# Attention and gated block on one core: outputs transposed straight into the operand of wo, head sets in pairs, and the order of every engine moved by a table

## Chip, core and metric

The kernel runs on one core of one Trainium2 chip. The metric is the device time of one execution in microseconds; several executions are timed, and their median counts. One further execution is recorded by the hardware profiler; its span and rows are what this document quotes.

## What is computed

The reference, cut to what matters (S = 2048 tokens, D = 640, 32 heads of 20, F = 1536, bf16):

```python
mod = (silu(c) @ w_mod).reshape(1, 6, 1, -1)          # sa, ca, ga, sb, cb, gb
h = layernorm(x) * (1 + ca) + sa
q, k, v = split_heads(h @ wqkv)
o = softmax(q @ k.T / sqrt(20)) @ v                   # every head, 2048 x 2048 scores
x = x + ga * (merge_heads(o) @ wo)
h = layernorm(x) * (1 + cb) + sb
x = x + gb * (((h @ w_gate) * (h @ w_up)) @ w_down)
```

The exponentials are the bulk of ScalarE's work: 32 heads x 2048 x 2048.

## The kernel before

**A planner writes the program.** `build_kernel` makes tasks (engine, modelled duration, dependencies, buffers), `Sched.run` lays them out by an event model with priorities and gates, and `emit_program` (L356) writes one instruction stream for each engine in that order, with semaphore waits for dependencies on other engines. Each engine then runs its list strictly in order. Constants such as QUADS, STAGE, D_LEAD, HOLD, PVTOL or FILL_MIN steer the plan; STAGE holds overrides by head set.

**Tiling.** Queries go in seven chunks (CHUNKS: one of 512, six of 256). A chunk has eight head sets of four heads, so 56 items; the last is cut into two halves of 128 (SPLITJ), 57 in all. An item's scores are made in units of 128 partitions (keys) x 512 columns: 2048 units in all. The four heads of a set lie in the four strips of 32 rows of TensorE.

**Two ways through the softmax.** Most units go to ScalarE (ACT): a score visit of PE (L1524) writes two units into one of two PSUM sets of two banks, ACT takes the exponential of both at once (L1561, 128 x 1024) into PP, and PE multiplies by V (L2192). QUADS says how many groups of four units of each item go to VectorE (DVE) instead: DVE adds a bias and writes int16 (DB, L1585), then splits exponent and mantissa (L1617, L1625), and the product of the two parts is made by GpSimd (POOL) in four pieces (L1637) or by DVE (L1622); each such unit takes two value passes on PE instead of one. Their scores ride on score visits, in one of four other PSUM banks (G: 5, 6, 2, 7), which also take the projections, the value sums and all other rounds. The matmuls of such rounds have the lines of two helpers, L970 (four column strips of 32) and L966 (the whole array, in the last suffix).

```python
QUADS = ((0, 4, 3, 3, 3, 4, 4, 4), (2, 2, 1, 2, 2, 2, 1, 2), ...
```

**End of an item** (`item_end_tasks`, L1707 on): DVE transposes the value sums in blocks of 32 (L1717, OT), takes the reciprocal of the row sums (L1723), POOL or DVE normalizes (L1725, OTn), DVE transposes back (L1734, OcT), and four or five DMAs per item on SP's queue (L1746) copy the rows of each head to their places in Ocp, the left operand of wo:

```python
t = dma("sp", nr * n * 2, f, dps, prio=1.05 if j >= NSET - 2 else 2, dur=720.0)
```

wo is loaded by one DMA (L1492); the last head set of the last chunk is taken out of OcT instead, against a copy of its rows of wo in wo7 (four small DMAs, L1493).

**Suffix of a chunk** (`suffix`, L1773 on), spread by gates over the next chunk's score visits: product with wo (L1827), second layer norm, transposes (L1889), gate and up products by column blocks of 128 of F, with the two products of a block side by side in one bank (L1959 copies the gate product, L1966 multiplies), down product (L2062), output. Weights of gate and up stream through three staging buffers (stg, L1931).

**First part.** Layer norm and projections of Q, K, V run beside the first chunk's scores. K and most of Q are packed, written to DRAM and read back in strips of 32 rows (KT<-k_rows L1289, QT<-q_rows L1298), all on SP's queue.

**Fillers.** Where the plan has PE idle and its recent activity low, it puts in matmuls with no result: products with zeros into a value bank (L2523) or with the identity (L2551, L2553).

Of the kernel before, what the change touches and what calls it, by code (L numbers as in the profile page):

```python
# [13 lines left out]
SEM = 60.0  # L14
# [4 lines left out]
X_FIRST = 0.0  # L19
ACT_LAT = 250.0  # L20
# [16 lines left out]
LKTOL = 300.0  # L37


class Task:  # L40
    __slots__ = ("head", "hval", "hknow", "eng", "dur", "lat", "deps", "emits", "ctr", "prio", "gate", "acq", "on_start", "slots",
                 "start", "done", "needed", "val", "know", "nleft", "ready", "users", "name", "mode", "seq", "rt", "sem",
                 "nbytes", "cond", "alt", "land", "firm", "lk", "dead", "key")

    def __init__(self, eng, dur, emits, deps=(), ctr=None, prio=0.0, lat=None, gate=0, acq=(), on_start=None,
# [28 lines left out]
        self.dead = False  # L74
        if lat is None:
            lat = {"pe": PE_DRAIN, "act": ACT_LAT, "dve": DVE_LAT, "pool": 60.0}.get(eng, 0.0)
        self.lat = lat

# [5 lines left out]
class Slots:  # L84

    def __init__(self, ids, name=""):
        self.name = name
        self.free = [(i, []) for i in ids]
        self.hold = {}
        self.gone = set()  # L90
        self.out = {}

    def avail(self, only=None):
        best = None
        for k, (i, rel) in enumerate(self.free):
# [3 lines left out]
            for r in rel:  # L99
                t = max(t, r.done + SEM)  # L100
# [16 lines left out]
    def done(self, i, task):  # L117
        h = self.hold[i]
# [9 lines left out]
    def add(self, i, rel):  # L128
        self.free.append((i, rel))


class Sched:

    def __init__(self):
# [28 lines left out]
        self.lk_last = None  # L163

# [39 lines left out]
    def _enable(self, task):  # L204
        t = 0.0
        for d in task.deps:
            t = max(t, d.done + SEM)
        task.rt = t
        heapq.heappush(self.pend[task.eng], (t, task.seq, task))
# [68 lines left out]
    def step_engine(self, eng):  # L278
        if self.free_at[eng] > self.t:
            return False  # L280
        self.pull(eng)
        rl = self.readyl[eng]
        for k, task in enumerate(rl):
# [5 lines left out]
            if self.locked(eng, task):  # L289
                continue  # L290
            if self.acquire(task, self.t):
# [63 lines left out]

def emit_program(nc, sched, nsem_dma=56):  # L356
# [23 lines left out]
    for t in sched.all:  # L380
# [11 lines left out]
        for d in deps:  # L392
            if not (d.nbytes or d.eng != eng or d.eng in ("dve", "pool")):
                continue
            if d.head and eng == "act":
# [88 lines left out]
TB_GATE = 2  # L484
# [3 lines left out]
D_LEAD = 0.451  # L488
NB0, NSS = 3, 3
XB0, XSS = 0, 0  # L490
HEADG = 1000
OP_EARLY = 1
EV_OP = 0.5
# [3 lines left out]
LN2T = 0.6  # L497
# [5 lines left out]
HOLD = 110  # L503
PVTOL = 249
XDPRIO = 1.343
# [5 lines left out]
STX_G, STX_T, STX_S, W_ISSUE = 3, 20, 1.5, 600.0  # L511
ZFILL = 1
WD_POOL, WD_PRIO = 1, 400.0
# [4 lines left out]
WM_GATE = 8  # L518
# [3 lines left out]
K_LEAD = 0.683  # L522
# [3 lines left out]
D_LATE = 16  # L526
D_RES = 20
PVMIN, PVMAX, PVCAP = 2, 7, 12
PV0 = 0
V_PARTS = [[0, 2], [2, 4], [4, 6], [6, 8]]  # L530
V_L1 = 0.2
# [10 lines left out]
GATE_F = (0.446, 0.5, 0.5, 0.5, 0.5, 0.5, 1.0)  # L542
FILL_MIN = 4190.746
# [9 lines left out]
LN2P = 0.85  # L553
NALT = 1
OPFIRST = 1500
STG_B = 0.95
ENDP, END3, P_POW = 0.4, 1, -1.0
HT_L = 0.25
V_L = 0.221
LATE_A = 2.065  # L560
LATE_L = 1.418
LATEQ = (2, 3)
LATEQ_A = -20
LATEQ_F = 0.35
# [2064 lines left out]
```

## Time and profile before

| | |
|---|---|
| median of 3 runs | 805.1 us (804.75 to 807.88) |
| span of the profiled execution | 803.8 us |
| instructions | 37,761 |
| DVE busy | 697.8 us |
| POOL busy | 386.0 us |
| data moved by DMA | 64.66 MB |

A row of the groups reads: line, engine, operation, output<-input, shapes, count; then busy time and the mean nanoseconds of one; then idle time of the engine just before, and what ended it. A row of a source line reads: minimum, median and maximum duration, then the first and last start. A row of stretches reads: the stretch, its length, busy time and count for PE, weight loads (PEld), DVE, ACT and POOL, then granted clock, DMA share and GB/s. A row of the chain or of the timeline reads: start, duration, what. "SPq" is a DMA's issue on SP's queue. ACT's time of one exponential covers its way through the engine, so neighbours overlap; the step from start to start says how fast they follow each other.

### The profile page before, as it was taken

The page shows a single profiled execution, that of the slowest core. Times are in us where ns is not written, and L with a number is a line of the kernel's source. Part 1 is how long each engine was busy: PE and PEld are TensorE (multiplying, and loading weights), DVE is VectorE, ACT ScalarE, POOL GpSimd, SP SyncE. Part 2 cuts the span into 40 slices and gives each one's busy share as a digit, 9 for nine tenths or more (in the row PEclk, how much of TensorE's full clock was granted, in tenths as well). Part 3 has the DMA queues.
Part 4 walks back from the last instruction along what each step waited for, and adds up shares of the span by engine and source line. Part 5 has one row for each costly group of instructions (what it writes and reads, how often), then busy time and mean ns, then how long its engine had stood idle before and what let it go on. Part 6 is the DMA issues. An engine that isn't in the chain of part 4 may idle for free.

```text
span 803.8 us, 37761 instructions
## 1 busy us (share of the span) xinstructions
PE 790.4 (98%) x16595; PEld 380.6 (47%) x16595; DVE 697.8 (87%) x1401; ACT 764.8 (95%) x847; POOL 386.0 (48%) x396
## 2 busy tenths in 40 slices
PE   8999999999999999999999999999999999999998
PEld 4433433333244434445555455555555555555567
DVE  7978788799989999988999999999899988898754
ACT  6899899999999999999999999999999999999961
POOL 3347455654366565763444443545534554455300
PEclk9999999999999999999999999999999999999999
DMA  9733212212341532120032404231540254414420
GB/s 297 243 113 91 62 43 64 61 33 76 92 109 50 167 88 52 35 55 13 24 81 65 95 16 112 57 73 39 121 89 15 54 118 94 98 37 106 92 68 18
DMA packets 154314, 64.66 MB, mean 80 GB/s; under 512 B 116951, under 2 KB 154151, under 8 KB 154151
## 3 DMA queue, kind: packets, MB, share of 16 engines
q1 hardware_dynamic: 153223, 61.10, 30.0%
q8 instruction: 132, 2.16, 1.1%
q10 hardware_dynamic: 928, 1.15, 0.5%
q14 instruction: 31, 0.25, 0.1%
HBM read 50.63 MB, written 8.99 MB: 74 GB/s over the span
## 4 chain that ended last, share of the span: by engine, by line
PE 77%; ACT 14%; DVE 5%; issue 2%; DMA 1%; SPq 1%; POOL 0%; DVEq 0%; ACTq 0%
PE ps_all L1524 26%; PE ps_all L970 21%; PE ps_all L2192 19%; ACT PP L1561 14%; PE ps_all L1230 4%; PE ps_all L966 3%; DVE DB L1585 2%; PE ps_all L1889 1%; PE ps_all L1166 1%; PE ps_all L1127 1%; DVE DSS L1617 1%; PE ps_all L2523 0%; DVE DSS L1625 0%; DMA QT<-q_rows 0%; PE ps_all L991 0%
## 5 line engine op out<-in xcount | busy, mean ns | idle before, releaser
L1561 ACT ACTIVATE PP<-ps_all 128x1024 bf16<-128x1024 f32 x810 | 748.5, 1090 | 6.7 <-PE ps_all L1524 4.8
L1637 POOL TENSOR_TENSOR DSS<-DB,DSS 128x512 bf16<-128x512 bf16 x268 | 305.0, 1157 | 290.6 <-DVE DSS L1625 254.2
L1585 DVE TENSOR_SCALAR DB<-ps_all 128x512 int16<-128x512 f32 x428 | 285.5, 681 | 50.5 <-PE ps_all L1524 48.0
L1524 PE MATMUL ps_all<-QT,KT 32*128 32x256 bf16 (+2 forms) x3648 | 319.4, 287 | 4.5 <-DMA QT<-q_rows 0.8
L1524 PEld LDWEIGHTS ps_all<-QT,KT 32*128 32x128 bf16 x3648 | 93.9, 92 | 204.1 <-ACT PP L1561 141.5
L2192 PE MATMUL ps_all<-PP,Vf 128*32 128x256 bf16 (+2 forms) x2892 | 163.6, 291 | 0.5 <-DVE KPB L1242 0.3
L970 PE MATMUL ps_all<-h2T,stg 128*32 128x256 bf16 (+2 forms) x2716 | 122.9, 281 | 0.3 <-DVE DB L1585 0.2
L2192 PEld LDWEIGHTS ps_all<-PP,Vf 128*32 128x32 bf16 (+1 forms) x2892 | 54.5, 94 | 76.4 <-issue 67.6
L2192 PE MATMUL ps_all<-DSS,Vf 128*32 128x256 bf16 (+1 forms) x1512 | 88.7, 291 | 0.0
L1617 DVE TENSOR_SCALAR DSS<-DB 128x2048 int16<-128x2048 int16 x107 | 77.2, 722 | 0.8
L970 PEld LDWEIGHTS ps_all<-h2T,stg 128*32 128x32 bf16 x2716 | 61.6, 96 | 26.9 <-issue 22.0
L1625 DVE TENSOR_SCALAR DSS<-DB 128x2048 int16<-128x2048 int16 x107 | 73.2, 684 | 0.8 <-PE ps_all L2192 0.8
L970 PE MATMUL ps_all<-wd,hprod 128*32 128x320 bf16 (+1 forms) x1404 | 61.0, 277 | 0.0
L1725 POOL TENSOR_TENSOR OTn<-OT,invT 128x256 bf16<-128x256 f32 (+1 forms) x49 | 35.3, 721 | 37.7 <-DVE invT L1723 37.5
L1622 DVE TENSOR_TENSOR DSS<-DB,DSS 128x2048 bf16<-128x2048 bf16 x40 | 51.5, 1287 | 0.0
L2192 PEld LDWEIGHTS ps_all<-DSS,Vf 128*32 128x32 bf16 x1512 | 36.5, 95 | 20.9 <-issue 12.4
L970 PE MATMUL ps_all<-wV,hT 128*32 128x160 bf16 x1280 | 38.9, 236 | 0.9 <-DVE DB L1585 0.3
L970 PEld LDWEIGHTS ps_all<-wd,hprod 128*32 128x32 bf16 x1404 | 31.2, 96 | 14.2 <-issue 10.8
L1717 DVE STREAM_TRANSPOSE OT<-ps_all 128x256 f32<-128x256 f32 (+2 forms) x57 | 27.1, 475 | 8.8 <-PE ps_all L2192 8.5
L1230 PE MATMUL ps_all<-hT,wk 128*32 128x512 bf16 x360 | 32.3, 382 | 0.0
L970 PEld LDWEIGHTS ps_all<-wV,hT 128*32 128x32 bf16 x1280 | 24.6, 97 | 15.9 <-issue 8.2
L1230 PE MATMUL ps_all<-hT,wq 128*32 128x512 bf16 x375 | 31.3, 382 | 0.6 <-DVE OT L1717 0.6
(133 smaller groups left out, 556.1 us busy)
## 6 DMA issues: line engine op xcount, KB each, us to landing
stg<-in_B_w_gate_dram SPq DMA_DIRECT2D x74, 160.0 KB
stg<-in_B_w_up_dram SPq DMA_DIRECT2D x74, 160.0 KB
KT<-k_rows SPq DMA_DIRECT2D x112, 32.0 KB
QT<-q_rows SPq DMA_DIRECT2D x48, 64.0 KB
Ocp<-OcT SPq DMA_DIRECT2D x164, 10.0 KB
wm<-in_w_mod_dram SPq DMA_DIRECT2D x3, 800.0 KB
x<-in_A_x_dram SPq DMA_DIRECT2D x7, 320.0 KB
k_rows<-KPA SPq DMA_DIRECT2D x16, 128.0 KB
```

What stands on the lines that cost most here:

```text
L970: return lambda e, b: e.matmul(ps[32 * x:32 * x + 32, b, c0 + o:c0 + o + w], lhs()[:, 32 * x:32 * x + 32], rhs() if w == n else rhs()[:, o ...
L1230: f = [lambda e, b_, k=k, x=x: e.matmul(ps[x:x + min(32, w - x), b_, :], wx[:, k, r0 + x:r0 + min(x + 32, w)], hT[tc][:, k, :], tile_posit ...
L1524: ems.append(lambda e, i=i, kt=kt: e.matmul(dstf()[:, i * u.n:(i + 1) * u.n], KT[32 * u.s:32 * u.s + 32, u.j, kt * 128:(kt + 1) * 128], QT ...
L1561: return e.activation(PPs[g % 2][:, cellp["p"], 0:nu * 512], ps[:, b0:b0 + nu, :].rearrange("p b c -> p (b c)"), AFT.Exp, scale=ESCALE)
L1585: return e.tensor_scalar(DBl[st_["slot"]][:, x * 512:(x + 1) * 512], bank(cell["b"]), EBIAS, 0.0, op0=ALU.add, op1=ALU.max)
L1617: return e.tensor_scalar(DSl[st_["ss"][0]][:, :], DBl[st_["slot"]][:, :], 0x7F, 0x3F00, op0=ALU.bitwise_and, op1=ALU.bitwise_or)
L1622: return e.tensor_tensor(d, DBl[st_["slot"]][:, :].bitcast(BF16), d, ALU.mult)
L1625: return e.tensor_scalar(DSl[st_["ss"][1]][:, :], DBl[st_["slot"]][:, :], 0x7F80, 2, op0=ALU.bitwise_and, op1=ALU.bitwise_or)
L1637: return e.tensor_tensor(d, DBl[st_["slot"]][:, x * w:x * w + w].bitcast(BF16), d, ALU.mult)
L1717: t1 = Task("dve", n * 1.1 + 70, lambda e: e.transpose(OT[:, 0:n], ps[:, item_info[it]["bank"], 0:n].rearrange("p (b q r) -> p b r q", q=3 ...
L1725: f3 = lambda e: e.tensor_tensor(OTn[:, 0:n].rearrange("p (b c r) -> p b r c", c=32, r=2), OT[:, 0:n].rearrange("p (b r c) -> p b r c", c= ...
L2192: ems.append(lambda e, i=i, kt=kt, stt=stt, stp=stp: e.matmul(ps[32 * s:32 * s + mc, bk, 0:u.n], Vf[:, (kt * H + 4 * u.j + s) * VW:(kt * H ...
```

## The change

What it does, beside new constants all over:

- **Outputs.** OcT, wo7 and the DMAs into Ocp go. The normalization writes only the 20 real columns of each head, head set beside head set, into one OTn of 160 columns per group of 64 queries. Once 32 columns are full, one transpose of DVE writes a block of Ocp. The rows of Ocp then have another order, and wo is loaded in 48 pieces to match.
- **Pairs.** Two neighbouring head sets of 256 queries share one bank of value sums, 256 columns each, and one first transpose, one reciprocal and one second transpose.
- **Gate and up** of two column blocks share a bank (256 columns each): one copy and one product of 512 instead of two of 256. Staging buffers: five, two of which open during the first chunks.
- **Score visits** are made when they are placed, from the next units in line with different strips, and P lives in sixteen single buffers. Sets of three banks exist in the code, but their gates (R1CH, MCH = 7) open only at the very end.
- **QUADS** is changed: 109 groups for DVE instead of 107.
- **Model.** The planner's latencies from engine to engine get corrections (LAT_X, REL_X, V_X, S_X), STAGE gets values for all 57 items.
- **Orders.** After the plan is made, `replan` takes 14 fillers out of PE's order and moves tasks of each engine by a table (1,499 of PE, 306 of SP, 182 of DVE, 25 of POOL, 1 of ACT), then lays the tasks out again for the semaphores.

```diff
-QUADS = ((0, 4, 3, 3, 3, 4, 4, 4), (2, 2, 1, 2, 2, 2, 1, 2), (2, 2, 1, 2, 2, 2, 1, 2), (2, 2, 1, 2, 2, 2, 1, 2), (2, 2, 1, 2, 2, 2, 1, 2), (2, 2, 1, 2, 2, 2, 1, 2), (2, 1, 2, 2, 2, 1, 2, 0))
+QUADS = ((0, 5, 3, 3, 3, 4, 3, 4), (2, 2, 2, 2, 2, 2, 1, 2), (1, 2, 1, 2, 2, 2, 1, 2), (1, 3, 1, 1, 2, 2, 1, 3), (2, 2, 1, 2, 3, 1, 1, 2), (2, 2, 1, 2, 2, 1, 2, 3), (2, 1, 2, 1, 1, 2, 4, 3))
...
+def replan(sc):
+    gone = set(PLAN.get("drop", ()))
+    sc.order["pe"] = [t for i, t in enumerate(sc.order["pe"]) if i not in gone]
+    for eng, moves in PLAN.items():
+        if eng == "drop":
+            continue
+        old = sc.order[eng]
+        gone = {a for a, _ in moves}
+        new = [t for i, t in enumerate(old) if i not in gone]
+        for a, b in moves:
+            new.insert(b, old[a])
+        sc.order[eng] = new
...
+PLAN = {
+    "drop": (1824, 1840, 2170, 2543, 3239, 3248, 3259, 3812, 3825, 4391, 4823, 5109, 5110, 5487),
+    "pe": [
+        (110, 113), (111, 114), (129, 128), (134, 133), (153, 145), (154, 146), (156, 147), (135, 149), (136, 150), (137, 151),
...
-    PPs = [alloc("PP", [128, NPS, w * 512], BF16) for w in ((3, 2) if HEADG < 1000 else (2, 2))]
-    wo7 = alloc("wo7", [128, D], BF16)
+    PP = alloc("PP", [128, NPP, 512], BF16)
...
-    d_wo = [dma("sp", 128 * KD * D * 2, lambda e: e.dma_start(wo_sb[:, :, :], wov[:, :, :]), [d_wm[3][0]], prio=10)]
+    d_wo = [[] for _ in range(KD)]
+    for j in range(NSET):
+        i0 = DH * j
+        while i0 < DH * j + DH:
+            i1 = min(DH * j + DH, i0 // 32 * 32 + 32)
+            for x in range(4):
...
+                d_wo[i0 // 32].append(dma("sp", (i1 - i0) * D * 2, fwo, [d_wm[3][0]], prio=10 + .01 * i0))
...
-        t4 = dve(n * .55 + 65, lambda e: e.transpose(OcT[:, cell["s"], 0:n].bitcast(F32), OTn[:, 0:n].bitcast(F32)), [t3],
-                 prio=pe_)
-        pcs = [] if direct else oc_pieces(j)
...
+        def f3(x):
+            return lambda e: e.tensor_tensor(
+                OTn[:, g0:g0 + gn, DH * (j + x):DH * (j + x) + DH, :].rearrange("p b c r -> p b r c"),
+                OT[:, nq_ * x:nq_ * x + nq_].rearrange("p (b r c) -> p b r c", c=32, r=2)[:, :, :, 1:1 + DH],
+                invT[:, 2 * gn * x:2 * gn * (x + 1)].rearrange("p (b r) -> p b r", r=2).unsqueeze(3).to_broadcast(
+                    [128, gn, 2, DH]), ALU.mult)
+        ds = [t2] + [y for x in range(nm) for b in range(DH * (j + x) // 32, (DH * (j + x) + DH - 1) // 32 + 1)
+                     for y in ot_read.get((ci - 1, b), [])]
...
+            def f4(e):
+                o = Ocp[slot][:, b0:b1, qo:qo + nq_].bitcast(F32).rearrange("p k (b c) -> p k b c", c=32)
+                i = OTn[:, g0:g0 + gn, 32 * b0:32 * b1, :].rearrange("p b (k c) r -> p k b (c r)", c=32).bitcast(F32)
...
+            t4 = dve(nq_ * nbk * .55 + 65, f4, dps, prio=pe_)
...
     sc.pick_pe = pick_pe
     end = sc.run()
     sc.nhalf = nhalf[0]
+    replan(sc)
     nw = emit_program(nc, sc)
```

More of the change, by code (lines that the diff above doesn't have):

```diff
@@ L496 @@
 TAIL_PRE = 1
-LN2T = 0.6
+LN2T = 0.177
 EAGER = 7
@@ L2137, in pv_candidates @@
                     break
+            elif it in lead and any(first_pv[(lead[it], s)] for s in range(4)):
+                break
             na = 0
```

931 lines of the change are left out of this document (614 added, 317 removed), and 227 rows, old and new, of the table PLAN.

## The prediction

> **What bounds the kernel now.** I read the page first: the busy shares, then the chain that ended last.
>
> ```profile
> span 803.8 us, 37761 instructions
> ...
> PE 790.4 (98%) x16595; PEld 380.6 (47%) x16595; DVE 697.8 (87%) x1401; ACT 764.8 (95%) x847; POOL 386.0 (48%) x396
> ...
> PE 77%; ACT 14%; DVE 5%; issue 2%; DMA 1%; SPq 1%; POOL 0%; DVEq 0%; ACTq 0%
> ```
>
> PE and ACT are both nearly full, and the chain runs mostly through PE. But a busy PE here is also a PE whose matmuls drain, so I asked next who sets the beat: the view of line 1561 (the exponentials), the chain between 160 and 190 us, the timeline of ACT at the end, and the waits of the weight loads.
>
> ```profile
> L1561 ACT ACTIVATE PP<-ps_all x810: 1002/1067/1327, 16.4 to 774.7; 128x1024 bf16<-128x1024 f32 x162
> ```
> ```profile
> 172.99 5.41 ACT PP L1561 x6
> ```
> ```profile
> 699.68 76.18 ACT L1561 ACTIVATE PP<-ps_all 128x1024 bf16<-128x1024 f32 x83
> ```
> ```profile
> PEld ps_all L1524 <- ACT PP L1561: 141.5, 479, 1.3
> ```
>
> 810 exponentials start between 16.4 and 774.7 us: 758.3 us for 809 steps, 0.937 us a step. Where the chain stays on ACT, six take 5.41 us, 0.902 each; I take that as the shortest step. Over the last 83 the step is (76.18 - 1.18) / 82 = 0.915 (1.18: 774.7 plus one exponential ends the row). 479 times the weight load of a score matmul waited for an exponential to release its banks: **ACT paces, PE follows closely behind.** So the span is 16.4 us of start, 809 steps, and 29.1 us from the last start to the end. At 0.902 the steps would take 729.7 us; the excess is 28.6 us. The table by stretch says where it lies.
>
> ```profile
> core 0: us, PE busy (x) PEld busy (x) DVE busy (x) ACT busy (x) POOL busy (x), PEclk, DMA share, GB/s
> 16.00:40.00 24.00, 23.49 (x447) 11.77 (x447) 22.70 (x65) 20.75 (x26) 9.13 (x21) 1.00 0.82 246
> 40.00:80.00 40.00, 39.53 (x651) 14.73 (x649) 32.06 (x59) 39.34 (x44) 23.42 (x21) 1.00 0.38 101
> 80.00:100.00 20.00, 18.93 (x375) 8.51 (x375) 14.32 (x32) 17.30 (x19) 10.18 (x9) 0.92 0.26 68
> 100.00:400.00 300.00, 296.78 (x5513) 119.42 (x5506) 270.90 (x496) 298.21 (x323) 167.53 (x158) 1.00 0.24 64
> 400.00:700.00 300.00, 298.74 (x7280) 158.47 (x7279) 275.27 (x546) 299.41 (x326) 139.99 (x142) 1.00 0.33 75
> 700.00:776.00 76.00, 74.68 (x1825) 40.08 (x1824) 56.30 (x118) 75.87 (x83) 29.72 (x31) 1.00 0.35 79
> ```
>
> A stretch counts what overlaps it, so I take one off each count. 80 to 100: 18 steps, 3.8 us over. 100 to 400: 322 steps of 0.932, 9.6 over; 400 to 700: 325 of 0.923, 6.9 over. 16 to 40 (some 20 exponentials among 26 instructions) is about 6 over. Between 80 and 100 us the chain and the clock name a cause:
>
> ```profile
> 87.61 0.76 SPq L1746
> ...
> 89.88 0.72 SPq L1746
> ...
> 90.71 3.51 DMA QT<-q_rows
> ...
> 94.78 1.30 DVE DB L1585 x2
> ```
> ```profile
> 96.00:100.00 4.00, 3.93 (x50) 1.24 (x50) 2.00 (x6) 3.18 (x4) 0.97 (x1) 0.61 0.01 4
> ```
>
> Four issues of Ocp<-OcT stand on SP from 87.61 to 90.60 ahead of the load of the next chunk's QT; PE waits for its landing and then loses clock (0.61 over 4 us, 1.6 us of full speed).
>
> **The change, part by part.**
>
> *Fewer exponentials.* QUADS gives DVE 109 groups of four units instead of 107 (the last entry of the last row is cut off by SPLITJ both times): 8 units leave ACT, 4 exponentials of two, 4 x 0.902 = **-3.6 us**. It costs PE two more value passes per group at some 0.4 us, covered by four score visits fewer.
>
> *Outputs straight into Ocp, and pairs.*
>
> ```profile
> L1746 SPq DMA_DIRECT2D Ocp<-OcT x248: 549/714/1642, 59.6 to 769.2; - x124
> L1493 SPq DMA_DIRECT2D wo<-in_A_wo_dram x4: 327/396/1384, 33.1 to 36.2; - x4
> L970 PE MATMUL ps_all<-wo,Ocp x656: 232/299/311, 228.8 to 699.7; 128*32 128x320 bf16 x116, 128*32 128x160 bf16 x48
> ```
> ```profile
> L1717 DVE STREAM_TRANSPOSE OT<-ps_all 128x256 f32<-128x256 f32 x47 | 20.8, 442 | 4.8 <-PE ps_all L2192 4.7
> L1717 DVE STREAM_TRANSPOSE OT<-ps_all 128x512 f32<-128x512 f32 x8 | 5.7, 712 | 1.4 <-PE ps_all L2192 1.3
> L1734 DVE STREAM_TRANSPOSE OcT<-OTn 128x128 f32<-128x128 f32 x47 | 14.2, 301 | 1.5 <-POOL OTn L1725 1.5
> L1725 POOL TENSOR_TENSOR OTn<-OT,invT 128x256 bf16<-128x256 f32 x42 | 27.9, 665 | 37.2 <-DVE invT L1723 37.0
> ```
>
> All 248 issues go, 177 us of SP's time, and with them the queue ahead of QT: I take **-3.0 us** (87.61 to 90.60) of the 3.8; bounds 0 and 3.8. Late next are the two DVE copies behind it on the chain (1.30 us at 94.78); the same late scores released them, and they keep the other 0.8. wo now comes in 48 pieces, not 5: 43 x 0.396 = 17 us more on SP, at most 43 x 1.384 = 60; the first use is at 228.8 us, and K and Q rows can go first, so nothing on the path; without that cover up to 17 us of late rows. DVE: pairs turn 46 first transposes of 256 into 23 of 512, 46 x 0.442 - 23 x 0.712 = -4.0 us; 57 second transposes become 31, 26 x 0.301 less and some of the rest wider, about -7.5 us; the wo7 product goes, and 13 narrow normalizations instead of 8 run on DVE, some +1. POOL normalizes 20 of 32 columns, 0.665 to some 0.45 us each (estimate, by elements), about -10 us, which lets it take a few more products. Added waits: the normalization waits for the previous chunk's transposes out of OTn, behind it stand POOL's products, whose PV can run half a head set later; a bank of G is held over two head sets. Both are hidden as long as PE has other rounds; at worst a fraction of a microsecond at each of the 34 ends that stay of 57.
>
> *Gate and up of two column blocks at once.*
>
> ```profile
> L1959 DVE CAST gsb<-ps_all 128x256 bf16<-128x256 f32 x60 | 24.6, 412 | 4.7 <-PE ps_all L970 4.6
> L1986 DVE CAST gsb<-ps_all 128x512 bf16<-128x512 f32 x12 | 8.1, 674 | 0.5 <-PE ps_all L970 0.5
> ```
>
> 60 casts and 60 products of 256 become 30 and 30 of 512: 120 x 0.412 - 60 x 0.674 = -9.0 us of DVE. Against that stand two groups more:
>
> ```profile
> L1585 DVE TENSOR_SCALAR DB<-ps_all 128x512 int16<-128x512 f32 x428 | 285.5, 681 | 50.5 <-PE ps_all L1524 48.0
> L1617 DVE TENSOR_SCALAR DSS<-DB 128x2048 int16<-128x2048 int16 x107 | 77.2, 722 | 0.8
> L1625 DVE TENSOR_SCALAR DSS<-DB 128x2048 int16<-128x2048 int16 x107 | 73.2, 684 | 0.8 <-PE ps_all L2192 0.8
> ```
>
> 2 x (4 x 0.681 + 0.722 + 0.684) = +8.3. DVE ends some 12 us lower, of 698. It isn't the pace, so this counts only through fewer small waits of PE, in the term of the orders. A round now needs two column blocks of weights before it starts, not one; five staging buffers (three before, two more once the projections are through) hold two such pairs. A round that waits for its second block holds up no score visit, since PE takes value passes in its place; what it costs without that cover is the wait, and I put both sides at nothing. P memory keeps its size: sixteen single buffers for eight double ones.
>
> *Fillers.*
>
> ```profile
> L2523 PE MATMUL ps_all<-ident,Vf 128*32 128x256 bf16 (+1 forms) x168 | 9.3, 301 | 0.0
> ```
>
> 168 matmuls, 8 or 4 to a filler; 14 fillers of at most 8 are 112 / 168 x 9.3 = 6.2 us of PE. They stand where PE waits for ACT; I take 0. Bounds: -6.2 if PE were the pace there, and above, 14 x 1.6 = +22 if each left a window of low clock like the one at 96 us. The Trainium skill ("TensorE: Matmul & The Clock Gate", Part 1: The HAM clock gate) says that an idle window of about 3.4 us halves the clock; the 0.61 above agrees in size. By that rule alone a gap of one filler, far shorter, costs nothing, and the sum stays.
>
> *Orders.* 1,499 tasks of PE change place (half by six places or less), 182 of DVE, 306 of SP, 25 of POOL, 1 of ACT. No row prices that. The nearest is the last stretch, 0.915 a step, with DVE least busy (56.30 of 76). If 100 to 700 ran so, it would gain 322 x 0.017 + 325 x 0.008 = **-8.1 us**, which I take, since DVE load falls and the moves are to small waits of this kind; bounds 16.5 (0.902 throughout) and, on the other side, a loss as in the third rival. The start to 40 us I leave, bounds -2 and +3: SP's first loads are reordered.
>
> *Tail.* One product (wo7) goes from the last two tiles:
>
> ```profile
> L966 PE MATMUL ps_all<-wo,OcT x4: 299/299/310, 773.8 to 778.2; 128*128 128x320 bf16 x4
> ```
>
> At most 1.0 us, half of it behind other matmuls: **-0.5**.
>
> Sum: 803.8 - 3.6 - 3.0 - 8.1 - 0.5 = 788.6 us of span. The median of the runs, 805.1, lies 1.3 over the profiled span, so **790 us**.
>
> **Rivals.**
>
> *The step stays.* If 0.92 is what ACT and PE together can do, the moves change nothing measurable: only -3.6 and -3.0 remain, 798.5 us. For it: ACT is busy 299.41 of 300 us from 400 to 700, and moved tasks are near their old places. Against it: 0.902 and 0.915 are both seen. The Trainium skill ("ScalarE: Activation LUTs", What ACT_TABLE_LOAD costs) gives 186 ns plus 0.833 ns per element, with some 93 ns of overlap between neighbours: an estimate of 946 ns for 1024 elements, so no excess at all would be left. The trace disagrees, at 0.902 a step.
>
> *The steps close up.* If the order takes out most of the 16.5 us between 100 and 700, another 8 us go, and some of the start: 780.
>
> *PE stands behind late results.* PE runs in order; a value pass moved ahead of a score visit waits if its exponential or DVE result comes later than the plan has it, and the score visit and ACT wait behind it.
>
> ```profile
> PEld ps_all L2192 <- DVE DSS L1625: 2.0, 9, 0.3
> ```
>
> Such a wait is 0.22 us now, nine times. It undoes the 15 us from some 70 waits on, of 1,499 moves; at 100 the time is 790 + 22 = 812. Against it: the plan's landings are later than before, so results should rather be early.
>
> **How the numbers follow.** Forecast 0.63 (784 to 796), step stays 0.19, steps close up 0.10, late results 0.08. A measurement of this kernel tells about 0.5% from no change, 801.1 to 809.1. Faster: 0.63 + 0.10 + two thirds of 0.19 (it reaches from 796 to 803) = 0.85; same 0.07; slower 0.08. The range from 779 to 803 leaves out most of the late results and the farther end of the closing up, about 0.13 in all, and takes in the bounds of the orders' term; the forecast's own is 784 to 796.
>
> **What would show it.** Right: some 806 exponentials, first start near 16.4, a mean step near 0.923; no Ocp<-OcT on SP and no excess over 1.5 us between 80 and 100, with the clock at 1.00; DVE near 685 us busy; 28.5 us from last start to the end. Wrong: a step still at 0.937 (rival one), new waits of PE for DVE or POOL in the list of waits (rival three), a first exponential after 19 us, or stretches of low clock where fillers were.

## The result, and the profile after

The changed kernel takes **826.1 us** (825.75 to 827.27), the kernel before 806.0 in the runs beside it (804.75 to 807.88): ratio **1.0241, 95% interval 1.0219 to 1.0264**. It is slower; 790 was forecast. The page of the profiled execution (825.75 us), its span, busy shares, granted clock and chain:

```profile
span 824.0 us, 37281 instructions
...
PE 789.6 (96%) x16536; PEld 377.0 (46%) x16536; DVE 699.9 (85%) x1276; ACT 759.7 (92%) x847; POOL 416.2 (51%) x416
...
PE   3599999999999999999999999999999999999998
...
PEclk8699999999999999999999999999999999999999
...
PE 51%; ACT 34%; issue 6%; DVE 4%; DMA 3%; SPq 1%; POOL 0%; ACTq 0%
```

PE and ACT have no more work than before (DVE has 2 us more, POOL 30), and past the second slice PE is as full as it was. The hole is in the first two slices, 40 us. The view of the exponentials' line says the same (x is the count, then shortest, median and longest, then first and last start):

```profile
L2939 ACT ACTIVATE PP<-ps_all x806: 1002/1164/1314, 38.0 to 792.3; 128x1024 bf16<-128x1024 f32 x162
```

The first exponential starts at 38.0 us, not at 16.4. From the starts of all exponentials in the two traces the span divides as follows; the excess is what the steps are longer than 0.9035 us, the step at which ACT follows itself in both. The third column is the first experiment below, the changed kernel with SP's first 17 issues in their old order.

| us | before | after | 17 issues put back |
|---|---|---|---|
| first exponential | 16.35 | **38.00** | 16.91 |
| steps at 0.9035 (809, 805, 805) | 730.9 | 727.3 | 727.3 |
| excess, first 100 steps | 12.2 | 12.0 | 11.5 |
| excess, steps 100 to 700 | 13.8 | 12.1 | 12.0 |
| excess, the rest | 1.4 | 2.9 | 3.1 |
| last start to the end | 29.1 | 31.7 | 31.7 |
| span | 803.8 | 824.0 | 802.6 |

The list of waits names what stood at the start (time in all, count, longest), and SP's timeline shows why (start, duration, then the issue):

```profile
PE ps_all L1394 <- DMA wm<-in_w_mod_dram: 19.3, 1, 19.3
```
```profile
7.53 2.11 SPq L1260 DMA_DIRECT2D x<-in_A_x_dram  x2
13.56 0.37 SPq L1271 DMA_DIRECT2D wV<-in_A_wqkv_dram  x1
15.28 0.37 SPq L1271 DMA_DIRECT2D wk<-in_A_wqkv_dram  x1
15.70 1.66 SPq L1260 DMA_DIRECT2D x<-in_A_x_dram  x2
20.96 0.37 SPq L1271 DMA_DIRECT2D wq<-in_A_wqkv_dram  x1
21.38 0.53 SPq L1260 DMA_DIRECT2D x<-in_A_x_dram  x1
21.95 0.47 SPq L1264 DMA_DIRECT2D wm<-in_w_mod_dram  x1
```

Of the kernel before, the same view:

```profile
1.18 0.42 SPq L857 DMA_DIRECT2D x<-in_A_x_dram  x1
1.64 0.46 SPq L861 DMA_DIRECT2D wm<-in_w_mod_dram  x1
```

This load brings the block of w_mod from which PE makes the shift sa (25 matmuls, L1394), one of the two modulations of the first layer norm. Without it the modulated x isn't complete, and neither K nor Q nor a score exists. The table has the entry `(2, 13)`: SP's third issue becomes its fourteenth. The loads that now go before it don't just take 0.5 us each. All but the first few carry a wait that the code gives them (`chain`: a load waits until the one that lies 900,000 bytes ahead in the code's order has landed), and a queue that runs in order makes the load of wm0, which has no such wait, stand through all of them. The chain of waits from 0 to 40 us shows these landings one after the other:

```profile
6.03 3.23 DMA x<-in_A_x_dram
...
9.28 5.99 DMA x<-in_A_x_dram
...
15.70 5.25 DMA x<-in_A_x_dram
...
21.95 7.20 DMA wm<-in_w_mod_dram
...
29.19 0.82 PE ps_all L1394 x25
```

And PE, with nothing to do, lost its clock (table by stretch; the clock is the third number from the end), so that what followed the landing ran slowly too (on the chain, the 20 transposes behind it took 2.13 us, and 1.14 in the kernel before):

```profile
0.00:20.00 20.00, 7.45 (x45) 2.79 (x45) 5.50 (x29) 4.87 (x11) 3.04 (x12) 0.82 0.76 234
20.00:40.00 20.00, 10.59 (x199) 6.59 (x199) 7.78 (x26) 7.43 (x14) 2.87 (x5) 0.66 0.28 84
```

Two smaller things are new. One step, at 542.7 us, is 2.7 us too long; ACT's and PE's timelines there:

```profile
546.29 1.94 ACT L2939 ACTIVATE PP<-ps_all 128x1024 bf16<-128x1024 f32 x2 [2.47 <-PE ps_all L2639]
```
```profile
544.21 1.49 PE L1373 MATMUL ps_all<-h2T,stg 128*32 128x256 bf16 x48
545.56 0.41 PE L2639 MATMUL ps_all<-DSS,Vf 128*32 128x256 bf16 x8
545.78 0.61 PE L2639 MATMUL ps_all<-PP,Vf 128*32 128x256 bf16 x16
```

The scores were there; the exponential waited 2.47 us for room in P memory, which the value passes at 545.78 gave, and these stood behind 48 matmuls of gate and up. The other is the tail. PE's groups after the last exponential's start, in the kernel before and in the changed one, differ in one row above all:

```profile
L970 PE MATMUL ps_all<-wd,hprodt 128*32 128x320 bf16 x48 | 2.2, 302 | 0.0
```
```profile
L1373 PE MATMUL ps_all<-wd,hprodt 128*32 128x320 bf16 x117 | 4.6, 300 | 0.0
```

69 matmuls of the down product that used to stand beside exponentials now stand after them: 2.4 of the 2.6 us.

### The profile page after: what moved, and what is told of

It reads as the page before. It is cut to its first block, busy times and chain, and to the rows that moved or that the text cites. A ratio compares the mean times of both kernels' runs of the same rounds, so it can differ in the third digit from the quotient of the medians.

```text
span 824.0 us, 37281 instructions
## 1 busy us (share of the span) xinstructions
PE 789.6 (96%) x16536; PEld 377.0 (46%) x16536; DVE 699.9 (85%) x1276; ACT 759.7 (92%) x847; POOL 416.2 (51%) x416
## 4 chain that ended last, share of the span: by engine, by line
PE 51%; ACT 34%; issue 6%; DVE 4%; DMA 3%; SPq 1%; POOL 0%; ACTq 0%
ACT PP L2939 34%; PE ps_all L1959 17%; PE ps_all L1373 16%; PE ps_all L2639 11%; PE ps_all L1369 3%; DMA x<-in_A_x_dram 2%; PE ps_all L1633 2%; DVE DB L1986 1%; DMA wm<-in_w_mod_dram 1%; DVE DSS L2022 1%; PE ps_all L1530 1%; DVE DSS L2030 0%; POOL DSS L2042 0%; PE ps_all L1569 0%; SPq L1692 0%
## 5 line engine op out<-in xcount | busy, mean ns | idle before, releaser
L2042 POOL TENSOR_TENSOR DSS<-DB,DSS 128x512 bf16<-128x512 bf16 x296 | 346.8, 1196 | 273.2 <-DVE DSS L2030 232.2
L2639 PE MATMUL ps_all<-PP,Vf 128*32 128x256 bf16 (+3 forms) x2876 | 161.6, 288 | 0.0
L1373 PE MATMUL ps_all<-h2T,stg 128*32 128x256 bf16 (+2 forms) x2808 | 114.1, 278 | 0.2 <-DVE DB L1986 0.2
L2639 PE MATMUL ps_all<-DSS,Vf 128*32 128x256 bf16 (+3 forms) x1544 | 96.6, 289 | 0.4 <-POOL DSS L2042 0.2
L2639 PEld LDWEIGHTS ps_all<-PP,Vf 128*32 128x32 bf16 (+1 forms) x2876 | 69.2, 95 | 45.6 <-issue 39.2
L2022 DVE TENSOR_SCALAR DSS<-DB 128x2048 int16<-128x2048 int16 x109 | 86.2, 790 | 2.2 <-PE ps_all L2639 0.6
L2030 DVE TENSOR_SCALAR DSS<-DB 128x2048 int16<-128x2048 int16 x109 | 76.0, 698 | 1.0 <-PE ps_all L2639 0.7
L2639 PEld LDWEIGHTS ps_all<-DSS,Vf 128*32 128x32 bf16 (+1 forms) x1544 | 39.9, 95 | 22.3 <-issue 16.9
L2124 POOL TENSOR_TENSOR OTn<-OT,invT 128x160 bf16<-128x160 f32 (+1 forms) x44 | 25.0, 588 | 31.0 <-DVE invT L2119 31.0
L1633 PE MATMUL ps_all<-hT,wk 128*32 128x512 bf16 (+1 forms) x360 | 31.3, 383 | 0.0
L1373 PE MATMUL ps_all<-wo,Ocp 128*32 128x320 bf16 (+1 forms) x660 | 29.1, 282 | 0.0
```

The source lines that it names most:

```text
L1373: return lambda e, b: e.matmul(ps[32 * x:32 * x + 32, b, c0 + o:c0 + o + w], lhs()[:, 32 * x:32 * x + 32], rhs() if w == n else rhs()[:, o ...
L1633: f = [lambda e, b_, k=k, x=x: e.matmul(ps[x:x + min(32, w - x), b_, :], wx[:, k, r0 + x:r0 + min(x + 32, w)], hT[tc][:, k, :], tile_posit ...
L2022: return e.tensor_scalar(DSl[st_["ss"][0]][:, :], DBl[st_["slot"]][:, :], 0x7F, 0x3F00, op0=ALU.bitwise_and, op1=ALU.bitwise_or)
L2030: return e.tensor_scalar(DSl[st_["ss"][1]][:, :], DBl[st_["slot"]][:, :], 0x7F80, 2, op0=ALU.bitwise_and, op1=ALU.bitwise_or)
L2042: return e.tensor_tensor(d, DBl[st_["slot"]][:, x * w:x * w + w].bitcast(BF16), d, ALU.mult)
L2124: return lambda e: e.tensor_tensor(OTn[:, g0:g0 + gn, DH * (j + x):DH * (j + x) + DH, :].rearrange("p b c r -> p b r c"), OT[:, nq_ * x:nq ...
```

## The experiments

Theory 1: the place of one load on SP's queue makes the loss. Rivals: the late start is partly given back later (A), or PE's moves make it (B). The table of moves stays otherwise unless a run says so.

**SP's first 17 issues put back (a1).**

```diff
             new.insert(b, old[a])
+        if eng == "sp":
+            new = old[:17] + [t for t in new if t not in old[:17]]
```

> The changed kernel, with SP's first 17 issues put back into their order of before the moves; all other moves stay. Theory 1 (the start): the load of wm0 was moved from SP's third place to its fourteenth, behind loads that wait for others to land; it went out at 21.95 us instead of 1.64, and the first exponential started at 38.00 us instead of 16.35. Then the first exponential comes back to 16.4 to 17.5 us, the steps and the tail stay as they are, and the time is 803 to 806 us. Rival A (the late start is partly given back): the rows of x and the weights that landed early behind the late wm0 spared stalls later; they return, and the time is 810 to 818 us with the first exponential at 16.4. Rival B (PE's own moves make the start late): the first exponential stays above 30 us and the time at 822 to 827 us.

Measured: 804.67 us, ratio to the kernel before 1.0005 (0.9987 to 1.0024). The first exponential is at 16.9:

```profile
L2941 ACT ACTIVATE PP<-ps_all x806: 1003/1166/1312, 16.9 to 770.9; 128x1024 bf16<-128x1024 f32 x162
```

21.1 of the 21.65 us of late start are gone, and of the span 21.4. Excess and tail are as in the changed kernel (table above), so nothing is given back: theory 1 holds, A and B fall.

**The load of wm0 alone put back (a4).**

```diff
+        if eng == "sp":
+            new.remove(old[2])
+            new.insert(2, old[2])
```

> The changed kernel with one move of SP undone: the load of wm0 goes out third again, every other issue keeps its moved place. Theory 1 in its narrow form (this one issue is the cause): first exponential at 16.4 to 18.5 us, time 803 to 807 us, within 2 us of the run with 17 issues put back. Theory 1 in its wide form (the swapped places of x, wk and wq count as well): first exponential at 19 to 23 us, time 807 to 812 us. Rival B (PE's moves): 822 to 827 us.

Measured: 807.56 us, 1.0042 (1.0019 to 1.0065); first exponential at 18.57 us, 1.7 later than with all 17. One issue is 19.4 of the 21.1 us, the swapped places of the others among the first 17 the rest. The first exponential lies just past the narrow form's range, the time in the wide form's: the one issue makes nearly all of it, not all.

**None of SP's moves (a2).** In `replan`: `if eng in ("drop", "sp"): continue`.

> The changed kernel without any of SP's 306 moves; moves of PE, DVE, POOL and ACT and the left-out fillers stay. Theory 1: the first exponential at 16.4 to 17.5 us. If SP's later moves are worth nothing, the time is that of the run with 17 issues put back, 803 to 806 us; if they cost, because loads that go out later hold up rounds of projections between 40 and 110 us (excess of 6 us there now), 797 to 802 us; if they pay, 807 to 812 us. Rival B: over 820 us.

Measured: 810.28 us, 1.0061 (1.0037 to 1.0084), first exponential at 16.83. So SP's later moves pay, against a1 5.6 us by the medians, 1.7 in the profiled executions. The profiled one had full clock and two longer steps, 1.2 us at 57.6 and 1.7 at 66.1; nine of ten runs had a mean clock of 0.992 to 0.998, one of ten in a1. So the rest goes with the clock; where it was lost isn't shown, since none of the slower executions was profiled.

**The late load alone, in the kernel before (b1, b2).** The first try moved an entry in a list from which emission takes only places:

```diff
+    o = sc.order["sp"]
+    o.insert(13, o.pop(2))
     nw = emit_program(nc, sc)
```

> The kernel before, with one edit: SP's third issue, the load of wm0, goes out fourteenth. Theory 1: the cost alone, put into a kernel that has nothing else of the change. The load goes out at about 18 us, behind wq's wait, lands some 7 us later and the first exponential starts about 9 us after that, as in the changed kernel (29.15 to 38.00): 31 to 35 us instead of 16.35, and the time is 820 to 825 us. Rival A (the start is mostly given back later): first exponential late, but the time below 814 us. Rival B (PE's moves made the start late): below 808 us.

Measured: 804.06 us, 0.9991 (0.9975 to 1.0006). In its trace the load of wm0 is still third, at 1.64 us. It tells nothing of the theories; it is the kernel before once more, and its interval shows what a comparison makes of no difference. Its profile shows the same for spans: 800.9 us, 2.9 below the profile of before, of which 2.3 lie in steps 60 to 100 and 0.6 in steps 100 to 700. In it the four issues of Ocp<-OcT stand ahead of QT just as they do in the prediction's rows, but PE never waits for QT, and the clock stays at 1.00:

```profile
86.35 3.56 SPq L1746 DMA_DIRECT2D Ocp<-OcT  x4
90.02 0.92 SPq L1298 DMA_DIRECT2D QT<-q_rows  x2
```
```profile
96.00:100.00 4.00, 3.88 (x87) 1.63 (x79) 3.04 (x6) 3.95 (x5) 1.20 (x2) 1.00 0.02 4
```

The second try put the changed kernel's `replan` into the kernel before, with this one move in place of the table.

> The kernel before with one edit: the load of wm0 is SP's fourteenth issue and not its third; every engine keeps its order otherwise (the run named b1 was to do this, but its edit changed a list that only names places, and its program is that of before: wm0 stands third in its trace, at 1.64 us). Theory 1: nothing but this place makes the start late. The load goes out at 17 to 19 us, behind the issues that wait for x and the weights, lands some 7 us later, and the first exponential starts some 9 us after that, at 32 to 36 us instead of 16.35; all of it stays, and the time is 819 to 824 us. Rival A (part is given back, because x and the weights are all there by then): first exponential as late, but the stalls of 5.8 us in the first 20 steps and 4.2 us between 80 and 100 us shrink, and the time is 810 to 817 us.

Measured: **820.37 us, 1.0201 (1.0184 to 1.0218)**. SP's timeline, and the line of the exponentials:

```profile
16.04 0.53 SPq L890 DMA_DIRECT2D wm<-in_w_mod_dram  x1
```
```profile
L1590 ACT ACTIVATE PP<-ps_all x810: 1003/1066/1328, 32.0 to 788.5; 128x1024 bf16<-128x1024 f32 x162
```

The load goes out at 16.04 us and not at 1.64, and the first exponential starts at 32.0, 15.65 us after that of before. The tail stays at 29.1, the excess is 25.6 us, between the 27.4 and the 24.4 of the two profiles of the kernel before, and by the medians 16.0 us are lost. Theory 1 holds, and nothing of A is shown. One place on one queue costs a kernel 2%. In the changed kernel the load goes out 5.9 us later still (21.95), behind loads that are swapped too, and the first exponential starts 6.0 us later (38.0).

**What the rest is worth: no table at all (a3).** The call of `replan` goes; the 14 fillers are in again.

> The changed kernel without its table: no moves on any engine, and the 14 fillers stay in. Everything else of the change (outputs straight into Ocp, pairs, two column blocks at once, groups) is there. First exponential at 16.4 to 17 us. If the table is worth what I forecast for the orders (8.1 us), the steps' excess over 0.9035 us is 8 us above the 26.7 us of the run with 17 issues put back, and the time 811 to 815 us. If it is worth nothing: 803 to 806 us. The stall of 2.67 us at step 537 and the tail of 31.7 us: if the table made them they go (29 us of tail, no step over 2 us past 100 us); if the groups and pairs made them, both are there too.

Measured: 808.96 us, 1.0065 (1.0036 to 1.0094), between the two ranges expected. The profiled execution is 6.6 us above that, with a stretch of low clock at 60 to 80 us (0.66), so only what lies past it is read: excess of steps 100 to 700 12.6 us, against 12.0 with the table and 13.8 before. The stall at step 537 is there with 3.0 us: the table did not make it. The tail is 32.9.

**Parts of the change undone, without the table.** Pairs off (`PAIRS = 0`); the last row of groups of before; all groups of before; one column block at a time (`GU2 = 0`):

> The changed kernel without its table, and with the head sets one by one again (PAIRS 0); to be read against the run without moves. Theory P (pairs pay, by some 4 us of DVE and fewer ends of a head set): 2 to 8 us slower than the run without moves, with more excess spread over the steps. Rival H (the bank that a pair holds over two head sets costs: exponentials wait for value passes that have no bank): the stall near step 537, if it is in the run without moves, goes, and the time is 1 to 4 us lower.

> The changed kernel without its table, and with the last row of the groups of before (2, 1, 2, 2, 2, 1, 2, 0): no groups of DVE in the last column, four fewer in all, two exponentials more. To be read against the run without moves. Theory G (the late groups make the tail: their products on POOL and their value passes end after the last exponential): the tail from the last exponential's start to the end is 2 to 3 us shorter, 28.5 to 29.5 us, and the time 0 to 1.5 us lower, since two more exponentials take 1.8 us. Rival W (PE's work decides: what the exponentials no longer cover is done after them): the tail is shorter only by about the 1.8 us that the last exponential comes later, and the time is the same within 1 us.

> The changed kernel without its table and with all groups of before (107, and 810 exponentials); to be read against the run without moves (808.96 us). If the new groups make the stall of 2.7 to 3.0 us at step 537, it goes. If the groups were worth the 3.6 us that the prediction gives to four exponentials fewer, the time is 811 to 815 us; the row of groups with only the last row undone took 815.6 us, by a longer tail, so that more than 815 us would put the last row's groups in the place that counts.

> The changed kernel without its table and with gate and up of one column block at a time (GU2 0); to be read against the run without moves (808.96 us). 60 more casts and products of DVE, some 9 us of it. If DVE's work has cover, as the prediction has it: 807 to 813 us, and the stall at step 537 goes if the pairs of column blocks made it. If fewer, wider rounds are what the change is worth: 815 to 825 us.

| without the table | us | ratio (95%) | last start to end | step near 537 |
|---|---|---|---|---|
| whole change (a3) | 808.96 | 1.0065 (1.0036 to 1.0094) | 32.9 | 3.0 over |
| pairs off | 823.06 | 1.0239 (1.0218 to 1.0261) | 39.7 | 2.6 over |
| last row of before | 815.55 | 1.0143 (1.0128 to 1.0158) | 38.4 | 3.0 over |
| groups of before | 821.32 | 1.0208 (1.0193 to 1.0224) | 41.0 | none |
| one block at a time | 824.44 | 1.0242 (1.0225 to 1.0259) | 38.6 | 8.6 over |

Theory G falls: without the late groups the tail is longer, not shorter. H falls too: the stall stays without pairs. It goes with the groups of before. The first two times lie outside every range expected, the last two inside one (above 815, and 815 to 825). But I don't read them as prices: the planner lays out every order anew, with constants found for the whole change, and each part less leaves a plan that ends badly, all with 5.5 to 8 us more of tail. PE's groups after the last start in the run with the last row of before:

```profile
L1373 PE MATMUL ps_all<-wd,hprodt 128*32 128x320 bf16 (+1 forms) x152 | 5.5, 298 | 0.0
L3132 PE MATMUL ps_all<-ident 128*32 128x512 bf16 x56 | 3.8, 381 | 0.0
```

More down product is left over, and 56 matmuls that only keep the clock are put into its gaps. I read this as constants and parts that fit each other. That isn't shown: no run had constants tuned for the smaller change, so that the parts are worth this much isn't ruled out.

**Who paces: PE's work doubled in places, ACT's work cut in places.** Both from a1.

```diff
+    for t in sc.order["pe"]:
+        if t.mode == "S" and t.name[1:].isdigit() and int(t.name[1:]) > 90 and int(t.name[1:]) % 8 == 4:
+            h = t.head or len(t.emits)
+            t.emits = t.emits[:h] + t.emits
+            t.head = t.head and 2 * h
```

> To be read against the run with SP's 17 issues put back, from which it differs in one thing: every eighth score visit after the 90th (89 visits) issues its score matmuls twice, with the same result. Two rounds of 256 columns more per visit, at 0.113 us each (40 matmuls of four rows took some 1.14 us of PE's chain at 522.6 us), are 0.23 us of PE a visit, 20 us in all. Theory A (ACT paces, PE has room; so the prediction has it): the time rises by 0 to 5 us. Rival E (PE's work paces: PE is busy for 98% of the span, and what the exponentials release only lengthens the tail): it rises by 15 to 22 us.

```diff
+                if nu > 1 and n > 90 and n % 8 == 4:
+                    return e.activation(PP[:, p[0]:p[0] + 1, :], ps[:, b0:b0 + 1, :], AFT.Exp, scale=ESCALE)
```

> To be read against the run with SP's 17 issues put back; leaves out half of every eighth exponential after the 90th (89 exponentials take 512 columns, not 1024; the other P block keeps its old values, and PE multiplies them all the same). ACT does some 89 x 0.43 = 38 us less; PE, DVE, POOL and SP do what they did, in the same order. Theory A (ACT paces): the time falls by 25 to 38 us. Rival E (PE's work paces): it falls by 0 to 6 us, and the last exponential starts earlier by no more than that, or the tail grows by what the exponentials gain. A mixture, each step by the later of the two: 8 to 20 us.

Measured: 812.36 us (1.0114, 1.0080 to 1.0148) with the doubled scores, 797.90 (0.9918, 0.9903 to 0.9933) with the halved exponentials. PE's row of the scores in a1, then with them doubled:

```profile
L1961 PE MATMUL ps_all<-QT,KT 32*128 32x256 bf16 (+2 forms) x3648 | 319.7, 286 | 7.7 <-ACT PP L2941 3.0 <-DVE DB L1988 0.8 <-DVE Vf L1731 0.4
```
```profile
L1961 PE MATMUL ps_all<-QT,KT 32*128 32x256 bf16 (+2 forms) x3986 | 337.7, 285 | 4.7 <-ACT PP L2941 2.0 <-DMA KT<-k_rows 0.6 <-DVE DB L1988 0.4
```

18.0 us more of PE cost 7.7 us by the medians, and 8.1 of excess. ACT's rows in the other run (busy, mean; then the idle time before):

```profile
L2943 ACT ACTIVATE PP<-ps_all 128x1024 bf16<-128x1024 f32 x716 | 673.3, 1038 | 24.9 <-PE ps_all L1961 14.7 <-PE ps_all L2641 5.7
L2941 ACT ACTIVATE PP<-ps_all 128x512 bf16<-128x512 f32 x90 | 57.2, 636 | 0.9 <-PE ps_all L1961 0.8
```

ACT was busy 24.0 us less (759.4 to 735.4) but waited 25.8 us before exponentials instead of 8.3 (a1's row); the span fell by 6.3. The 24.0 understate what was taken from ACT, since neighbours that no longer follow at once overlap less: the shortest step behind a halved exponential is 0.494 us in this trace, 0.41 below the full one, 36 us for 89. Neither theory A nor E, and less than the mixture expected: the two engines pace together. A microsecond of ACT alone is worth a sixth of one (6.3 / 36; a quarter by busy time), a microsecond of PE four tenths (7.7 / 18.0). The tail grew by only 0.4 us.

**Fillers and the small softmax (d1, d2, d3, b3).** d3 puts the 14 fillers of the changed kernel back into a1. d2 moves the softmax of c ahead of the passes of xn (`o.insert(5, o.pop(7))` on ACT, `o[19:25] = o[22:25] + o[19:22]` on DVE), d1 leaves out all fillers beside that, b3 takes the fillers past 100 us out of the kernel before.

> The run with SP's 17 issues put back, with the 14 fillers back in their places; all else as there. If leaving them out was worth PE's time, as the lower bound of the prediction has it: 2 to 6 us slower. If they stood where PE waits for ACT: within 1 us. If they kept the clock up: the clock is 1.00 in that run without them, so that a gain by them would need a stretch that is not there; 0.

> The run with SP's 17 issues put back, with the small softmax of c (one exponential of ACT, two small operations and one product of DVE) ahead of the passes of xn. There wm1's columns start at 8.73 us, behind scol at 8.50; in the kernel before scol stood at 6.68 and the columns started at 7.99, when wm1 had landed. The first exponential should start 0.4 to 0.8 us earlier, at 16.1 to 16.5 us instead of 16.91, and the time be 0.4 to 0.8 us lower, some 804.0 us; if xn's passes are the later ones, nothing changes.

> The run with SP's 17 issues put back, with two edits: the small softmax of c stands ahead of the passes of xn on ACT and DVE (as in the run d2), and all fillers are left out (40 matmuls of 3.6 us of PE in that run's profile, 36 of them between 56 and 76 us). If PE's work paces where they stand: the time falls by the softmax's 0.6 us and by up to 3 us more, 801 to 804 us, and it is a version that is below both kernels. If they keep the clock up: a stretch of low clock between 56 and 80 us, and the time rises by 2 to 7 us. If they only fill gaps of PE: as d2.

> The kernel before without its fillers past 100 us (16 fillers of 8 or 4 matmuls, 128 by 256 columns, in two clusters at 171 to 188 and 695 to 707 us and singly between); the ones at 46 to 70 us stay. Theory E (PE's work paces, fillers are work): the time falls by 1.5 to 3 us (112 such matmuls cost some 2.4 us in the changed kernel), to 801.5 to 803 us, and the clock stays at 1.00. The prediction's reading (they stand where PE waits for ACT): within 0.5 us. If they keep the clock up: stretches of low clock near 180 or 700 us, and 1 to 10 us slower.

| | us | ratio (95%) | mean clock, span of the profiled run |
|---|---|---|---|
| d3, 14 fillers in | 807.08 | 1.0014 (0.9997 to 1.0030) | 1.000, 805.3 |
| d2, early softmax | 804.91 | 0.9989 (0.9969 to 1.0009) | 1.000, 803.5 |
| d1, d2 with no fillers | 807.21 | 1.0022 (1.0002 to 1.0042) | 0.987, 810.6 |
| b3, before without late fillers | 807.35 | 1.0033 (1.0015 to 1.0052) | 0.992, 805.3 |

Leaving out the 14 fillers gained 1 to 3 us: 0.7 by the ratios of d3 and a1, whose intervals overlap, 2.7 by their profiled spans. Of these, 1.5 lie in steps 100 to 700 (13.5 of excess against 12.0), which five profiles without these fillers (the changed kernel, a1, a2, a4, d2) repeat within 0.1 us. The softmax gained nothing; the first exponential starts at 16.77 instead of 16.91. The fillers that the change kept pay (without them 2.3 us more, d1 against d2), and so do those of before past 100 us (2.1 us, b3). The table by stretch of d1, then of b3:

```profile
60.00:64.00 4.00, 4.00 (x52) 1.14 (x45) 3.48 (x5) 3.40 (x4) 1.15 (x1) 0.64 0.26 71
64.00:68.00 4.00, 3.40 (x28) 0.89 (x29) 3.94 (x8) 3.66 (x5) 2.24 (x3) 0.50 0.84 254
```
```profile
701.00:702.00 1.00, 0.47 (x8) 0.11 (x4) 1.00 (x3) 1.00 (x3) 0.00 (x0) 1.00 0.00 1
702.00:703.00 1.00, 0.82 (x22) 0.47 (x22) 1.00 (x3) 1.00 (x3) 0.49 (x1) 1.00 0.00 0
703.00:704.00 1.00, 0.48 (x12) 0.11 (x4) 1.00 (x3) 1.00 (x3) 0.92 (x2) 0.88 0.00 0
704.00:705.00 1.00, 0.99 (x18) 0.50 (x22) 1.00 (x4) 1.00 (x2) 0.61 (x2) 0.50 0.00 0
```

In b3 the cluster of 695 to 707 us was missing, the clock went to 0.50 at 704, and the steps from 700 on took 3.7 us more than before. Theory E's gain of 1.5 to 3 us didn't come; the third case did, a low clock and a loss of 2.

d2 is 2.5% below the changed kernel and not to be told from the kernel before. No version that does all of the work was found below both.

## Why the prediction was wrong

**The step that failed is "The start to 40 us I leave, bounds -2 and +3: SP's first loads are reordered."** The start cost +21.65 us (a1: 21.1 of it from the order of SP's first 17 issues; b2: 16 us from one issue). The move stood in the table as `(2, 13)`, and the timeline of before showed what it moved: the third issue, at 1.64 us, with the modulation columns right behind its landing. Working it out was possible, from the kernel before alone: its load of wq, the issue that would stand ahead, goes out at 18.17 us; the other wm load took 6.7 us to land; and from wm0's columns at 9.44 to the first exponential at 16.35 are 6.9. 18.6 + 6.7 + 6.9 = 32.2 us, and b2 measured 32.0. That it is so near is luck: in b2 the load went out at 16.04, 2.5 us earlier than this, and from its columns to the first exponential were 9.2 us, not 6.9, with the clock at 0.79 from 20 to 40 us. In the changed kernel, where the loads ahead are swapped too, it is 38.0. I sized the step by the 0.5 us that an issue takes, not by the waits that the issues passed carry. None of my rivals was this case; "a first exponential after 19 us" stood in the list of what would show me wrong.

The other terms, by the same rows:

- *Fewer exponentials, -3.6.* There are 806, and the steps are 3.6 us shorter in sum. But the step counted ACT's time as the kernel's, and c_half_exp shows what that is worth: some 36 us off ACT brought 6.3, so that 3.6 would bring some 0.6 (an estimate from that run). The tail took 2.6 us more, as work of PE that no exponential covers now; that the four exponentials fewer put it there isn't shown, and with all groups of before the tail was longer still (41.0, without the table).
- *No issues of Ocp ahead of QT, -3.0.* The issues are gone, of QT's landing one wait of 0.5 us is left (98 to 128 us), and the clock is 1.00 from 100 to 120 us. Yet steps 60 to 100 are still 4.2 us over (4.9 before), so -0.7. Even that rests on one execution: in the other profile of the same program (b1) these steps are 2.6 us over, with the same issues ahead of QT. So the term was mis-sized: it counted the 3.0 us of the issues, where the profile of before has one wait of PE for QT of 0.8 us and the 1.6 us of clock behind it, about the 2.3 by which the two profiles differ in these steps, and the other profile has neither. The late result in that place is not a DVE copy, as I had it, but PE: 84 matmuls with wmb, in the kernel before and after,

```profile
L970 PE MATMUL ps_all<-wmb,SCb x84: 233/299/310, 83.0 to 89.1; 128*32 128x320 bf16 x76, 128*32 128x160 bf16 x8
```
```profile
L1373 PE MATMUL ps_all<-wmb,SCb x84: 232/299/311, 106.7 to 111.8; 128*32 128x320 bf16 x76, 128*32 128x160 bf16 x8
```

  run beside projections in just these steps, and the value passes that make room in P memory stand behind them: the largest excess of after there, 2.0 us, is at 108.6 us, and the list of waits from 98 to 128 us has

```profile
ACT PP L2939 <- PE ps_all L2639: 3.0, 2, 1.9
```

  That the column products cause it is read off the order of the rows; no run moved them.
- *Orders, -8.1.* From step 100 to 700 the excess fell by 1.7 us, with the new stall of 2.7 in it, and without any move by 1.2 (a3). With the 14 fillers in, as a3 has them, the table's excess there is 13.5 (d3), 0.9 more than without it: in the stretch where I put the gain the moves by themselves gain nothing, and the fall against the kernel before comes with the rest of the change and with the fillers left out. What the table pays, 1.9 us by the medians of d3 and a3 and 4.1 by their ratios, must lie in the first 100 steps and in the tail (31.7 against 32.9).
- *Fillers, 0.* -1 to -3 us, within the bounds.
- *Tail, -0.5.* It is +2.6, as shown: I looked at the product that goes, not at the 69 matmuls of the down product that now stand there (2.4 us).
- *DVE some 12 us lower* (the terms add up to 11.2). 699.9 us, 2 more than before. Without the table it is 682.7 (a3), 15 lower; see the last section. POOL, for which I had -10, has 30 more (416.2): normalizing took 10 less, but there are 296 products and not 268, each 39 ns longer.
- *Rival three* (PE behind late results): not a hundred small waits, but a few long ones at ACT. Exponentials waited for value passes three times, 5.5 us in all, where the kernel before has one such wait of 1.2; the passes were late in PE's own order.

So with the start mended the change is worth -1.2 us of span: +0.6 start, -3.6, -0.7 excess, +2.6 tail. That is less than the 2.9 us by which two profiles of the kernel before differ, and by the medians it is nothing (1.0005). Of the 15.2 us that the forecast summed up, the orders' 8.1 were not there, the 3.0 ahead of QT were mostly not there, and of ACT's 3.6 little can be kept while PE paces too.

## What to carry to other kernels

A queue that issues in order makes every issue stand through the waits of all issues ahead of it: before a transfer is moved back, list what the ones that it passes wait for, and ask which chain starts at its landing. Where two engines are both over 95% busy, price a saving on one at a fraction (here between a sixth and four tenths), and look for the rest in waits for the other. Before a term is built on one stall in one profile, see whether a second execution has it. A part taken out of a plan whose constants were found for the whole is no clean price of the part: the fit of the constants goes with it.

## What the hardware showed that I had not expected

**The clock falls without a long gap.** From 698 to 704 us of b3 PE was busy 47 to 82% of each microsecond, and its longest wait there was 0.53 us; still the clock was at 0.50 from 704 on. The Trainium skill ("TensorE: Matmul & The Clock Gate", HAM oscillation — how this bites in real kernels) gives as the abstract rule that PE must have no idle gap above some 3.4 us; by that rule b3 should have kept its clock, and the measurement decides against it. The next section of the page (A second HAM failure mode: psum-queue depth-cycling) tells of a clock that swings because PE idles briefly and often. The trace agrees in that short idles were enough; the cycling of PSUM banks to which the page puts them down isn't shown here. In the prediction I used the gap alone, though no window of 3.4 us was idle ahead of its 0.61 either: PE was busy for 3.00 of the 4 us from 92 to 96.

**The same DVE instruction took 12% longer with the table.** DVE's row in the changed kernel, then in the run without moves:

```profile
L2022 DVE TENSOR_SCALAR DSS<-DB 128x2048 int16<-128x2048 int16 x109 | 86.2, 790 | 2.2 <-PE ps_all L2639 0.6
```
```profile
L2022 DVE TENSOR_SCALAR DSS<-DB 128x2048 int16<-128x2048 int16 x109 | 76.6, 703 | 1.1 <-PE ps_all L2639 0.4
```

POOL's products rose as well, from 1156 to 1196 ns. The Trainium skill ("SBUF — State Buffer", SBUF: two separate sides) says that a GpSimd instruction and a DVE instruction of some kinds (in a two-port mode, or with two inputs from SBUF) take turns on one pair of ports, each for the whole instruction. The traces agree with such a lock: with the table 71 of these 109 have no POOL instruction beside them, take 686 ns on the mean and never over 697, and the 38 others take 986, up to 1,722; without the table 91 take 681 and 18 take 813. So the rise lies in the ones that run beside POOL, and there are 20 more of them. Whether this instruction is of the kinds that the page names isn't shown, and no run moved POOL's work by itself.
